# A factor of one and a half on the planned loads of MoE2's x, and the order searched anew with operations that either of two engines can take

## The chip, the cores and the metric

The kernel runs on one core of a Trainium2 chip. The metric is the device time of one execution in microseconds (us), lower is better. The five engines run their own instruction lists in order and wait for each other by semaphores: PE (TensorE, matrix products), DVE (VectorE), ACT (ScalarE), POOL (GpSimd), and SP (SyncE), which here issues nearly all DMA transfers. PEld in a profile is PE's loading of weights, which runs beside its products.

## The reference

Attention with a threshold, then two feed-forward blocks ("MoE" and "MoE2", each one expert), all in float32:

```python
scores = scale * q @ k.T                       # 4 batches, 8 heads, 576 x 576, head size 64
thresh = max(scores, -1) - tau
attn = softmax(where(scores >= thresh, scores, -1e9))
x = (attn @ v) as 2304 tokens x 512
h = x @ w1_in                                  # 512 -> 2048
x = (h * clip(h + 3, 0, 6) / 6) @ w1_out       # 2048 -> 512
h = x @ w2_in
out = (h * sigmoid(1.702 * h)) @ w2_out
```

## The kernel before

Products in float32 are made from parts in the format fp32r: each operand is split into a high part (a rounding copy, by ACT) and a low part (a subtraction, by POOL or DVE), and three products of parts (high x high, high x low, low x high) are accumulated. The first four attention units use plain float32 products, the others the split. Weights come as 64-bit patterns and are decoded first (L482: two ACT copies, three DVE operations, one POOL addition), then split (L514).

**Stages.** Attention has 16 units (4 batches x 4 pairs of heads). For a unit: scores S on PE (L663, L679, L695), maximum R on DVE (L711), threshold `th` (L712), exponential on ACT (L714), masking and sum on DVE (L715), normalisation of `e` on POOL (L728), transposition of `e` on PE (L769) with the copy to `et` on ACT (L772), product with v on PE (L811, L828), result `xr`, and its split into `xh` and `xl`. MoE1's first half of the hidden width (`moe_a`, products L888 and L913) is worked in between the units, so that PE has work while the softmax chains run. Then come the second half of MoE1 (`moe_b`, and `wide` with L1003 and L913), and MoE2 in five blocks of tokens, twice, once for each half of the hidden width. For MoE2's first product two blocks of 256 tokens and 256 columns are combined, so that seven products do instead of eight (L1101, PE line L1114); its x is read back from DRAM as two tiles, xa and xb (`halves`, L1044, loads at L1050), differences of them are made on DVE (L1056), and each of the seven operands is split (L1060: high part on ACT, low part `outlring` on DVE).

**What sets the order.** Nothing in the order is written out by hand. Each operation is added to a plan with an engine, a cost in ns, a nominal time and its buffers. `order` (L135) is a list scheduler: it plays the plan with these costs, with gaps between engines (LAT, L24), four PSUM banks, at most eight transfers at a time, and the rule that DVE and POOL do not hold their common port at once (PORT). `settle` (L260) alternates it with a backward pass, then perturbs the priorities by a list of random seeds (KICKS, SHAKES); what is left at the end is the order in which instructions are issued. A negative number in these lists exchanges an operation's engine for its alternative, where it has one (`alt`). Before the change SHAKES holds 264 seeds and no negative number. A transfer costs bytes / 360 ns (L403), with a factor for some kinds: 1.5 for weights (L504), 1.4 and 1.5 for the first k and q (L617, L614), none for MoE2's x.

**Padding.** `fill` (L290) walks through PE's planned list and, where the plan's PE stands still and a PSUM bank is free, puts in products of a constant tile `two` (L1281), which nothing reads:

```python
count = int((s - t) / 450 if s < 12000 else (s - t - 300) / 216)
```

Of the kernel before, what the change touches and what calls it, by code (L numbers as in the profile page):

```python
# [18 lines left out]
P = 128  # L19
# [37 lines left out]
)  # L57


# [275 lines left out]
def tile_top_attention_moe_moe2(  # L335
# [13 lines left out]
    nc = tc.nc  # L349
# [42 lines left out]
    def add(eng, cost, time, name, fn, rd=(), wr=(), touch=(), alt=None):  # L392
        op = pl.add(eng, cost, time, fn, rd, wr, name, touch)
        op.alt = alt
        for c, names in changed:
            if any(b.pool in names for b in op.bufs):
                op.deps.add(c)
        return op

    def move(time, name, nbytes, fn, rd=(), wr=(), eng=SP):  # L400

        op = add(eng, 590, time, name, fn, rd, wr)
        add(DMA, nbytes / 360, time, name, lambda: None, rd, wr).deps.add(op)  # L403

    def buf(tag, ring, pool, shape, dt=F32):
        return Buf(pl, tag, ring, lambda: pools[pool].tile(shape, dt, tag=tag, name=tag, bufs=ring), pool)
# [27 lines left out]
    def f32(ap):  # L434
        return ap.bitcast(F32)
# [4 lines left out]
    def act(n):  # L440
        return 51 + 0.834 * n

    def dve(n):
        return 69 + 1.042 * n
# [4 lines left out]
    def pool2(n):  # L449
        return 160 + 2.13 * n  # L450

    def copy(o, i, **kw):
        return lambda: nc.scalar.activation(out=o(), in_=i(), func=ACTF.Copy, **kw)  # L453

    def tt(eng, o, a, b, op):
        return lambda: (nc.vector if eng == DVE else nc.gpsimd).tensor_tensor(out=o(), in0=a(), in1=b(), op=op)  # L456

    dram = ctx.enter_context(tc.tile_pool(name="dram", bufs=1, space=bass.MemoryType.DRAM))
    x1d, ypd, x2d, y2d = (dram.tile([DM, NT], F32, name=n) for n in ("x1d", "ypd", "x2d", "y2d"))
# [584 lines left out]
    def halves(c0, n, whole, K):  # L1044

        T = n if whole else 2 * n
        xa, xb = (buf(x, 1, "xs", [P, 2, 512]) for x in ("xa", "xb"))
        src_b = [x2d_b[b, p] for b, p in x2d_b if b * S + CH[p][0] < c0 + T and c0 < b * S + sum(CH[p])]
        for i, x in enumerate((xa, xb)):
            move(K("LX"), "LX", 8 * P * T, lambda i=i, x=x: nc.sync.dma_start(out=x.t[:, :, :T], in_=x2d[i * 2 * P:(i + 1) * 2 * P, c0:c0 + T].rearrange("(k p) t -> p k t", p=P)), src_b, [x])  # L1050

        def part(x, i=0):
            return lambda: x.t[:, :, i:i + n]

        def minus(o, a, b, rd, wr):
            add(DVE, dve(2 * n), K("XD"), "XD", tt(DVE, o, a, b, ALU.subtract), rd, wr)  # L1056

        out_ = []

        def put(i, src, rd):  # L1060
            h, l = (buf("out" + x + "ring2", HF, "ring2", [P, DM], F32R) for x in "hl")

            def v(x):
                return x.t[:, :2 * n].rearrange("p (k n) -> p k n", k=2)

            add(ACT, 93 + act(2 * n), K("XHC") + i, "XHC", copy(lambda: v(h), src), rd, [h])
            eng = XENG[i]
            add(eng, pool2(2 * n) if eng == POOL else dve(2 * n), K("XLC") + i, "XLC", tt(eng, lambda: v(l), src, lambda: f32(v(h)), ALU.subtract), rd + [h], [l])
            out_.append((h, l))

        put(0, part(xa), [(xa, 0)])
        if whole:
            put(1, part(xb), [(xb, 0)])
            return out_
        t1, t2 = (buf("xt", 2, "xs", [P, 2, 256]) for _ in range(2))
        minus(part(t1), part(xa, n), part(xa), [xa], [t1])
        put(1, part(t1), [t1])
        put(2, part(xb), [(xb, 0)])
        minus(part(t2), part(xb, n), part(t1), [(xb, 1), t1], [t2])
        put(3, part(t2), [t2])  # L1080
        put(4, part(xb, n), [(xb, 1)])
        minus(part(xa, n), part(xa, n), part(xb, n), [(xb, 1)], [(xa, 1)])
        put(5, part(xa, n), [(xa, 1)])
        minus(part(xb), part(xb), part(t2), [t2], [(xb, 0)])
        put(6, part(xb), [(xb, 0)])
        return out_
# [65 lines left out]
    def moe2(c0, T, f0, w, t0, last):  # L1152
# [4 lines left out]
        def K(name, i=0):  # L1157
            return t0 + dt * i + NOMINAL[name]

        xs = halves(c0, n, whole, K)  # L1160
        pys = [buf(f"py{c}", 1, "py", [P, 512]) for c in range(KC)]

# [14 lines left out]
        for c in range(KC):  # L1177
# [15 lines left out]
            else:  # L1193
# [6 lines left out]
                   T=5000, DT=4000, DM=4700, EF=5400, EH=5500, EL=6000, AV=7000, RB=8500, BT=9000, XR=9400, XM=9600, XH=10000, XL=10500, ST=10000, H=0, RL=1500, GT=2000, GH=2500, GL=3000,  # L1200
# [4 lines left out]
    t, u = 0, 0  # L1205
    for b in range(B):
        halves_ = []
        for j in range(H // 2):
            halves_.append(unit(u, b, j, t))
            if u < FULL:  # L1210
                halves_[j](0)
                t, u = t + 2700 * 4, u + 1
            else:
                halves_[j]()
                t, u = t + 2700 * 9, u + 1
# [124 lines left out]
```

## Time and profile before

| | |
|---|---|
| device time, 3 runs | 1059.94 to 1062.44 us, median 1061.24 us |
| the profiled execution | 1058.04 us, span of its instructions 1056.3 us |
| busy in it | PE 1043.3, PEld 948.3, DVE 730.1, ACT 629.6, POOL 511.3 us |
| granted clock of PE | 1.00 throughout |
| DMA | 141.72 MB, 134 GB/s in the mean |

A share of busy time is a mean over stages with different limits, and PE's padding counts as busy. In the view by windows a row gives each engine's busy time and instruction count in that stretch. In a timeline each row has the start, the duration, the engine, line and operation, and in brackets the idle time before it with what ended it. A line number can be that of a helper: L453 is every ACT copy, L456 every subtraction, addition or multiplication of two tensors. One float32 product of the program leaves two rows in the trace (padding L1281, L679, L695).

### The profile page before, as it was taken

How to read it: one execution, taken by the hardware profiler on the slowest of the kernel's cores; microseconds unless marked ns; L12 is line 12 of the kernel's file. 1: busy time of each engine (PE TensorE's matmuls, PEld its weight loads, DVE VectorE, ACT ScalarE, POOL GpSimd, SP SyncE). 2: the span in 40 equal slices, each digit the busy share in tenths (PEclk: the TensorE clock that was granted, in tenths of full speed). 3: DMA queues.
4: the chain of work that ended last, by engine and by line, in shares of the span. 5: the costliest groups of instructions: out<-in, count | busy, mean ns of one | idle time of the engine just before them, and what ended most of it. 6: DMA issues, size and time to landing. Idle time of an engine off the chain costs nothing.

```text
span 1056.3 us, 19440 instructions
## 1 busy us (share of the span) xinstructions
PE 1043.3 (99%) x7084; PEld 948.3 (90%) x7084; DVE 730.1 (69%) x1502; ACT 629.6 (60%) x1240; POOL 511.3 (48%) x581
## 2 busy tenths in 40 slices
PE   8999999999999999999999999999999999999998
PEld 6687888899889998999999999889988998989988
DVE  8988888767878782688865434997687577464534
ACT  5999676666767664766553225656665576345433
POOL 4688888776867663765573217431322232001000
PEclk9999999999999999999999999999999999999999
DMA  8334565645564535455743303446554342321302
GB/s 249 102 114 141 151 172 162 184 132 164 161 184 132 152 111 162 133 148 169 229 136 124 102 28 115 134 125 204 169 181 129 125 157 77 117 85 37 95 11 66
DMA packets 83648, 141.72 MB, mean 134 GB/s; under 512 B 8160, under 2 KB 47712, under 8 KB 82016
## 3 DMA queue, kind: packets, MB, share of 16 engines
q1 hardware_dynamic: 83408, 140.18, 43.8%
q8 instruction: 56, 0.92, 0.4%
q14 instruction: 40, 0.33, 0.1%
q10 hardware_dynamic: 144, 0.29, 0.1%
HBM read 97.32 MB, written 43.12 MB: 133 GB/s over the span
## 4 chain that ended last, share of the span: by engine, by line
PE 90%; DVE 4%; POOL 3%; issue 2%; ACT 1%; DMA 0%; POOLq 0%; DVEq 0%; ACTq 0%
PE py L913 27%; PE pm L1114 16%; PE pm L888 11%; PE pm L913 8%; PE pm L1003 7%; PE pm L828 6%; PE ps L663 5%; PE pm L769 5%; PE pm L811 2%; PE ps L695 1%; POOL e L728 1%; POOL kqv L456 1%; DVE e L715 1%; DVE nm L711 1%; PE pm L1281 1%
## 5 line engine op out<-in xcount | busy, mean ns | idle before, releaser
L913 PE MATMUL py<-g,outhring 128*128 128x512 f32 (+3 forms) x1024 | 279.8, 357 | 1.8 <-DVE g L456 0.7
L913 PEld LDWEIGHTS py<-g,outhring 128*128 128x128 f32 x1024 | 177.9, 188 | 18.2 <-DVE g L456 1.9
L913 PE MATMUL py<-g,outlring 128*128 128x512 f32 (+3 forms) x512 | 182.5, 356 | 0.0
L1114 PE MATMUL pm<-outlring,inhring 128*128 128x256 f32 x512 | 144.0, 281 | 1.2 <-DVE outlring L456 1.2
L1114 PE MATMUL pm<-outhring,inhring 128*128 128x256 f32 x512 | 144.3, 282 | 0.0
L1114 PE MATMUL pm<-outhring,inlring 128*128 128x256 f32 x512 | 143.8, 281 | 0.0
L711 DVE TENSOR_REDUCE nm<-ps 128x1 f32<-128x576 f32 x144 | 107.0, 751 | 42.4 <-PE ps L663 36.4
L715 DVE SCALAR_TENSOR_TENSOR e<-ps,th,e 128x576 f32<-128x576 f32 x128 | 102.5, 811 | 17.8 <-ACT e L714 15.8
L456 POOL TENSOR_TENSOR g<-t,g 128x256 fp32r<-128x256 f32 (+2 forms) x88 | 83.4, 953 | 63.1 <-ACT g L453 50.2
L714 ACT ACTIVATE e<-ps,nm 128x576 f32<-128x576 f32 x128 | 93.2, 738 | 32.4 <-DVE nm L711 27.0
L456 POOL TENSOR_TENSOR wmstg<-wmstg,wrstg 128x512 uint32<-128x512 uint32 x48 | 65.9, 1373 | 96.3 <-DVE wmstg L510 57.6
L456 POOL TENSOR_TENSOR g<-tc,g 128x512 fp32r<-128x512 f32 x24 | 32.2, 1341 | 162.6 <-ACT g L453 160.8
L913 PE MATMUL pm<-g,outhring 128*128 128x256 f32 (+1 forms) x512 | 106.8, 300 | 0.0
L913 PEld LDWEIGHTS py<-g,outlring 128*128 128x128 f32 x512 | 96.2, 188 | 10.9
L1114 PEld LDWEIGHTS pm<-outlring,inhring 128*128 128x128 f32 x512 | 96.7, 189 | 5.4 <-DVE outlring L456 1.5
L1114 PEld LDWEIGHTS pm<-outhring,inhring 128*128 128x128 f32 x512 | 96.7, 189 | 4.6 <-ACT u L453 0.4
L888 PE MATMUL pm<-xh,inhring 128*128 128x256 f32 (+1 forms) x320 | 97.5, 305 | 0.2
L1114 PEld LDWEIGHTS pm<-outhring,inlring 128*128 128x128 f32 x512 | 97.5, 190 | 0.0
L888 PE MATMUL pm<-xh,inlring 128*128 128x256 f32 (+1 forms) x320 | 94.5, 295 | 0.0
L888 PE MATMUL pm<-xl,inhring 128*128 128x256 f32 (+1 forms) x320 | 94.4, 295 | 0.0
L772 ACT ACTIVATE et<-pm 128x512 f32<-128x512 f32 (+2 forms) x144 | 75.1, 557 | 17.1 <-PE pm L769 14.6
L913 PEld LDWEIGHTS pm<-g,outhring 128*128 128x128 f32 x512 | 82.1, 189 | 0.5 <-issue 0.5
(122 smaller groups left out, 2461.1 us busy)
## 6 DMA issues: line engine op xcount, KB each, us to landing
turned<-tr SPq DMA_DIRECT2D x12, 1024.0 KB, 3.9
et<-turned SPq DMA_DIRECT2D x48, 256.0 KB, 6.2
wrawstg<-in_w1i_dram SPq DMA_DIRECT2D x16, 512.0 KB, 4.0
wrawstg<-in_w1o_dram SPq DMA_DIRECT2D x16, 512.0 KB, 3.6
wrawstg<-in_w2i_dram SPq DMA_DIRECT2D x16, 512.0 KB, 4.2
wrawstg<-in_w2o_dram SPq DMA_DIRECT2D x16, 512.0 KB, 4.1
qk<-in_k_dram SPq DMA_DIRECT2D x24, 288.0 KB, 3.6
qk<-in_q_dram SPq DMA_DIRECT2D x24, 288.0 KB, 3.8
```

Of the source, the lines that this page charges most:

```text
L456: return lambda: (nc.vector if eng == DVE else nc.gpsimd).tensor_tensor(out=o(), in0=a(), in1=b(), op=op)
L663: nc.tensor.matmul(ps.t[:, i, :SH], qss[hd].t[:, q0:q0 + P], w[hd].t[:, i * SH:(i + 1) * SH], start=a, stop=z)
L711: add(DVE, 672, K("R", s), "R", lambda: nc.vector.tensor_reduce(out=nm.t[:, c], in_=ps.t[:, :, :SH], op=ALU.max, axis=AX.XY, negate=True), ...
L714: add(ACT, 624, K("X", s), "X", lambda: nc.scalar.activation(out=ev(), in_=ps.t[:, :, :SH], func=ACTF.Exp, bias=nm.t[:, c]), [ps, (nm, s)] ...
L715: add(DVE, 736, K("M", s), "M", lambda: nc.vector.scalar_tensor_tensor(out=ev(), in0=ps.t[:, :, :SH], scalar=th.t[:, c], in1=ev(), op0=ALU ...
L769: nc.tensor.transpose(pt.t[:kn, o:o + P], e_of[s].t[:, keys(k)], id_b.t)
L772: add(ACT, act(size), K("EH", at), "EH", lambda: nc.scalar.activation(out=dst(kn)[0], in_=dst(kn)[1](pt.t[:kn, :size]), func=ACTF.Copy), [ ...
L828: nc.tensor.matmul(pv[p].t[64 * hd:64 * hd + 64, :CH[p][1]], v_(k, hd), x, start=k == 0, stop=k == 4)
L888: nc.tensor.matmul(ph.t[:, :n], a, v, start=(cc == 0 and i == 0), stop=(cc == KC - 1 and i == 2))
L913: nc.tensor.matmul(py.t[:, :n], a, v, start=(st and i == 0), stop=(sp and i == 2))
L1003: nc.tensor.matmul(ph.t[:, :n], a, v, start=(cc == 0 and q == 0), stop=(cc == KC - 1 and q == 2))
L1114: nc.tensor.matmul(o.t[:, :n], u.t[:, ws], v.t[:, xv], start=(st and kk == 0 and i == 0), stop=(sp and kk == 1 and i == 2), skip_group_che ...
```

## The change

The cost of the two loads of x for each MoE2 block is multiplied by 1.5 in the plan; the transfers are the same. SHAKES keeps its 264 seeds and gets 319 numbers more, of which 136 are negative: they exchange engines, some operations more than once, and 108 operations end on their alternative engine.

```diff
@@ SHAKES
-    461089389, 641840093, 940935001, 302617623, 395272555, 1040798833, 496012712, 151625592, 914921461,
+    461089389, 641840093, 940935001, 302617623, 395272555, 1040798833, 496012712, 151625592, 914921461, 827017900, -3099, -737, -1052, 639256428, 818694334, 148551951,
...
@@ halves
-            move(K("LX"), "LX", 8 * P * T, lambda i=i, x=x: nc.sync.dma_start(
+            move(K("LX"), "LX", 8 * P * T * 1.5, lambda i=i, x=x: nc.sync.dma_start(
...
```

In the built program DVE goes from 1360 instructions to 1390, ACT from 1243 to 1235, POOL from 586 to 564, SP stays at 487, and PE has 56 padding products where it had 34. Lines of the changed kernel are 18 higher than those of the kernel before.

**Start, DVE's list.** Rows around the seventh and eighth score tiles; before:

```order
L711 TENSOR_REDUCE nm<-ps 128x1
L715 SCALAR_TENSOR_TENSOR e,sm<-ps,th,e 128x576
L712 TENSOR_SCALAR th<-nm,nt 128x1
L623 TENSOR_SCALAR kqv<-kqv,sc 128x384
L507 TENSOR_SCALAR wmstg<-wmstg 128x512
L619 TENSOR_SCALAR g<-g,sc 128x512
L715 SCALAR_TENSOR_TENSOR e,sm<-ps,th,e 128x576
L711 TENSOR_REDUCE nm<-ps 128x1
L509 TENSOR_SCALAR wmstg<-wmstg 128x512
L712 TENSOR_SCALAR th<-nm,nt 128x1
```

The same place in the changed kernel:

```order
L729 TENSOR_REDUCE nm<-ps 128x1
L733 SCALAR_TENSOR_TENSOR e,sm<-ps,th,e 128x576
L730 TENSOR_SCALAR th<-nm,nt 128x1
L791 COPY et<-pm 128x512
L525 TENSOR_SCALAR wmstg<-wmstg 128x512
L733 SCALAR_TENSOR_TENSOR e,sm<-ps,th,e 128x576
L729 TENSOR_REDUCE nm<-ps 128x1
L740 RECIPROCAL rc<-sm 128x4
L527 TENSOR_SCALAR wmstg<-wmstg 128x512
L729 TENSOR_REDUCE nm<-ps 128x1
```

A copy of transposed `e` out of PSUM, which ACT made before, stands in DVE's list, and a threshold is missing from it (it is on ACT).

**Entry into MoE2, POOL's list.** `g<-t` are low parts of MoE1, `g<-tc` those of MoE2, `inlring` low parts of weights; before:

```order
L456 TENSOR_TENSOR g<-t_849,g 128x432
L456 TENSOR_TENSOR inlring_8183<-ws,inhring_8161 128x512
L456 TENSOR_TENSOR inlring_8271<-wmstg_8052,inhring_8180 128x256
L456 TENSOR_TENSOR inlring_8182<-wmstg_8063,inhring_8160 128x512
L456 TENSOR_TENSOR g<-tc,g 128x512
```

The same place in the changed kernel:

```order
L474 TENSOR_TENSOR g<-t_872,g 128x432
L474 TENSOR_TENSOR wmstg_8111<-wmstg_8111,wrstg_8180 128x512
L474 TENSOR_TENSOR g<-tc,g 128x512 x2
L474 TENSOR_TENSOR inlring_8458<-wmstg_8096,inhring_8442 128x256
L474 TENSOR_TENSOR inlring_8456<-wmstg_8111,inhring_8405 128x512
L474 TENSOR_TENSOR inlring_8457<-ws,inhring_8425 128x512
```

The three low parts of the last pair of weights stand behind the first two `g` of MoE2, no longer ahead of them.

**Entry into MoE2, SP's list** of transfers; before:

```order
L496 DMA wrawstg_8019<-in_w2i_dram 128x4x256
L496 DMA wrawstg_8087<-in_w2o_dram 128x1024
L496 DMA wrawstg_8109<-in_w2o_dram 128x1024
L1050 DMA xa<-x2d 128x2x512
L1050 DMA xb<-x2d 128x2x512
```

The same place in the changed kernel:

```order
L514 DMA wrawstg_8067<-in_w2i_dram 128x4x256
L514 DMA wrawstg_8130<-in_w2o_dram 128x1024
L1068 DMA xa<-x2d 128x2x512
L1068 DMA xb<-x2d 128x2x512
L514 DMA wrawstg_8185<-in_w2o_dram 128x1024
```

The loads of the first block's x have moved ahead of one load of weights.

## Rows read from the trace of the kernel before

**Rows 1.** The page's first part: busy time, share of the span, instructions.
```profile
PE 1043.3 (99%) x7084; PEld 948.3 (90%) x7084; DVE 730.1 (69%) x1502; ACT 629.6 (60%) x1240; POOL 511.3 (48%) x581
```

**Rows 2.** Windows: length, then busy (count) of PE, PEld, DVE, ACT, POOL; clock; DMA.
```profile
0.00:5.00 5.00, 3.62 (x17) 3.62 (x18) 1.25 (x9) 1.28 (x1) 3.99 (x20) 1.00 0.40 115
5.00:54.30 49.30, 46.33 (x295) 33.76 (x294) 46.91 (x116) 39.77 (x73) 26.77 (x35) 1.00 0.60 179
54.30:420.00 365.70, 363.30 (x2767) 319.25 (x2768) 273.06 (x679) 254.20 (x499) 269.56 (x364) 1.00 0.53 152
420.00:650.00 230.00, 229.64 (x1420) 225.58 (x1418) 143.32 (x240) 113.70 (x217) 120.22 (x98) 1.00 0.44 133
650.00:750.00 100.00, 97.36 (x651) 90.72 (x650) 81.93 (x142) 62.86 (x129) 36.37 (x27) 1.00 0.48 150
750.00:1053.00 303.00, 302.96 (x1942) 275.36 (x1940) 183.23 (x318) 157.73 (x323) 54.40 (x41) 1.00 0.32 103
1053.00:1056.30 3.30, 0.10 (x1) 0.00 (x0) 0.42 (x1) 0.00 (x0) 0.00 (x0) 1.00 0.24 79
```

**Rows 3.** Windows of the padding (L1281) alone: length, then PE and PEld busy.
```profile
0.00:5.00 5.00, 3.62 (x16) 3.49 (x16) 1.00 0.40 115
5.00:54.30 49.30, 4.04 (x29) 3.59 (x28) 1.00 0.60 179
54.30:420.00 365.70, 3.48 (x24) 3.19 (x24) 1.00 0.53 152
```

**Rows 4.** The chain that ended last, around 37 and 54 us: start, length, what.
```profile
37.31 0.14 DVE th L712
37.46 1.21 PE ps L679 x4
...
54.30 2.06 PE pm L888 x15
```

**Rows 5.** Timeline of DVE at the start, between 27 and 31 us.
```profile
27.90 0.68 DVE L510 SCALAR_TENSOR_TENSOR wmstg<-wrawstg,wmstg 128x512 uint32<-128x512 uint32 x1
28.50 0.81 DVE L715 SCALAR_TENSOR_TENSOR e<-ps,th,e 128x576 f32<-128x576 f32 x1
...
29.91 0.42 DVE L507 TENSOR_SCALAR wmstg<-wmstg 128x512 f32<-128x512 f32 x1
30.24 0.21 DVE L712 TENSOR_SCALAR th<-nm,nt 128x1 f32<-128x1 f32 x1
30.36 0.41 DVE L456 TENSOR_TENSOR xr<-xr,pm 128x256 f32<-128x256 f32 x1
```

**Rows 6.** Timelines of DVE and of POOL around 24 us.
```profile
23.78 1.43 DVE L623 TENSOR_SCALAR kqv<-kqv,sc 128x384 f32<-128x384 f32 x1
...
23.50 1.49 POOL L456 TENSOR_TENSOR inlring<-wmstg,inhring 128x512 fp32r<-128x512 f32 x1 [0.92 <-ACT inhring L453]
```

**Rows 7.** Timelines of SP, ACT, DVE, POOL and PE at the entry into MoE2.
```profile
659.86 0.38 SPq L1050 DMA_DIRECT2D xa<-x2d  x1
...
665.20 0.63 ACT L453 ACTIVATE outhring<-xa 128x512 fp32r<-128x512 f32 x1 [1.16 <-DMA xa<-x2d]
...
667.62 1.76 DVE L456 TENSOR_TENSOR outlring<-xt,outhring 128x512 fp32r<-128x512 f32 x1
669.31 0.68 DVE L456 TENSOR_TENSOR outlring<-xb,outhring 128x512 fp32r<-128x512 f32 x1
...
666.22 2.62 POOL L456 TENSOR_TENSOR inlring<-wmstg,inhring 128x256 fp32r<-128x256 f32 x2 [1.68 <-ACT inhring L453]
...
669.44 0.39 PE L1114 MATMUL pm<-outlring,inhring 128*128 128x256 f32 x1 [1.23 <-DVE outlring L456]
```

**Rows 8.** The view of tile xa: time from issue to landing of its ten loads.
```profile
DMA to landing us min/median/max: 2.8/3.8/5.3
```

**Rows 9.** Who PE waited for from 54.3 to 420 us: total, times, longest.
```profile
PE pm L769 <- ACT et L772: 0.9, 2, 0.7
PE pm L769 <- POOL e L728: 0.5, 2, 0.3
```

More of the change, by code (lines that the diff above doesn't have):

```diff
@@ L1049, in halves @@
         for i, x in enumerate((xa, xb)):
-            move(K("LX"), "LX", 8 * P * T, lambda i=i, x=x: nc.sync.dma_start(out=x.t[:, :, :T], in_=x2d[i * 2 * P:(i + 1) * 2 * P, c0:c0 + T].rearrange("(k p) t -> p k t", p=P)), src_b, [x])
+            move(K("LX"), "LX", 8 * P * T * 1.5, lambda i=i, x=x: nc.sync.dma_start(out=x.t[:, :, :T], in_=x2d[i * 2 * P:(i + 1) * 2 * P, c0:c0 + T].rearrange("(k p) t -> p k t", p=P)), src_b, [x])
         def part(x, i=0):
```

18 rows, old and new, of the table SHAKES are left out of this document.

## Prediction

> **What bounds the kernel now.** I read the page's line of busy times first, then the window view by stage, the padding alone in the same windows, the chain, and last the timelines of the two places where TensorE stands still. TensorE (PE) is busy for 1043.3 of the 1056.3 us [rows 1], and no operation of PE's real work is touched by the change. What an order can win is only what PE does not spend on that work: 1056.3 - 1043.3 = 13.0 us of idle time, and the padding matmuls on `two`, which count as busy. The window view splits the idle time: 1.4 us before the first matmul, 3.0 us from 5 to 54.3 us, 2.4 us from 54.3 to 420, 0.4 us from 420 to 650, 2.6 us from 650 to 750, nothing from 750 to 1053, and 3.2 us behind the last matmul [rows 2]. Padding adds 3.6, 4.0 and 3.5 us in the first three stretches [rows 3]. Head, first loads and tail (1.4 + 3.6 + 3.2) no order removes. So three places count: the start with 7.0 us, the attention stage with 5.9 us, the entry into MoE2 with 2.6 us. They cannot give more than about 16 us together, and the last 300 us give nothing, though x of MoE2 is loaded there for six more blocks.
>
> At the start the chain runs through VectorE's (DVE's) list until 37.5 us and then through PE, up to the first matmul of MoE1 at 54.3 us [rows 4]. DVE is busy for 46.9 of the 49.3 us before that matmul, ScalarE (ACT) for 39.8 [rows 2]. An operation that joins DVE there delays nearly everything behind it.
>
> At the entry PE waits 1.23 us for a low half of x that DVE makes. That subtraction took 1.76 us, the next one of the same size 0.68, and GpSimd (POOL) ran two weight subtractions, 2.62 us together, over just that time. Before it, ACT waited 1.16 us for xa [rows 7].
>
> **The change part by part.** The added factor changes no transfer; it alters what the plan believes, and with the new numbers the whole program is put into another order. What can be costed is what stands in the orders.
>
> *Entry into MoE2.* xa is issued at 659.86, before and after the change behind the last weights of w2i; but in the new order one of the two w2o loads stands behind xa and xb, not ahead. ACT got xa at 665.20, 5.3 us after its issue [rows 7]; the ten loads of xa took 2.8 to 5.3 us with a median of 3.8 [rows 8], so up to 1.5 us comes back there. POOL's two subtractions that blocked DVE now stand behind two `g` of MoE2, which cannot run before the first products are done. PE has three more output matmuls as cover, too. The 1.23 us should vanish, and about half of the remaining 1.4 us of that stretch is of the same chain: I take a quarter of it, 0.35. Term: **-1.6 us**, ends -2.6 (all idle time of the stretch) and 0 (the load is still late).
>
> *Start.* Up to the fourth `xr` multiply, which releases MoE1's first matmul, DVE has the same list as before but for these: two copies of 128x512 out of PSUM and one of 64x128 come from ACT, one subtraction of 128x512 comes from POOL, one cast of 128x512 comes from ACT, and three thresholds `th` of 128x1 go to ACT. DVE's step is read from start to start: an operation of 128x512 on two inputs 0.60 us, a one-input operation of that size 0.33, `th` 0.12 [rows 5]. The copies' PSUM source is not in these rows, so I price them like the 0.60 and the small one at 0.2, between `th` and 0.33. Sum: 3 x 0.60 + 0.33 + 0.2 - 3 x 0.12 = **+2.0 us**. What hid the copies before was ACT, idle for 9.5 of those 49.3 us; that cover is spent for nothing by moving them to the fuller engine. Lower end 0: ACT's share shrinks by as much, and if it was ACT that held the pace anywhere, DVE's idle 2.4 us take the rest. Upper end from the padding: the new order has 37 padding matmuls ahead of MoE1's first one, the old 22. The program puts one only where the plan's PE stands still, and each leaves two rows in the trace: 29 rows took 4.04 us [rows 3], 0.14 us a row, so 15 x 2 x 0.14 = +4.2 us.
>
> The rows show that a DVE operation can be held by POOL: a scaling of `kqv` took 1.43 us while POOL subtracted for 1.49 us [rows 6], against 0.42 for a one-input operation of 512 elements [rows 5]. The Trainium skill, SBUF — State Buffer, section SBUF: two separate sides, has the rule: DVE and GpSimd share one pair of ports under an exclusive lock, and DVE operations in a two-port mode or with two SBUF inputs wait for the whole GpSimd instruction. By it the two newcomers at the start with SBUF sources alone could each wait about 1.0 us (1.43 - 0.42), and the start would cost +4.0 instead of +2.0; the trace agrees with the rule at these places. I keep +2.0, because moving the subtraction also takes 1.3 us of work from POOL there, and the sum's upper end holds the other value anyway.
>
> *Attention stage, 54.3 to 420 us.* In the whole program 32 `th` move from DVE to ACT; 13 copies of transposed `e`, 27 other copies and casts, two scalings, 10 normalisations and 14 subtractions move to DVE; four clamps of weights go from DVE to POOL. Most of this lies in this stage. DVE is the fuller helper here (273 us of 366, against 254 and 270 [rows 2]) and has room for them. What PE visibly waited for is an ACT copy of `et` (0.9 us) and a POOL normalisation (0.5 us) [rows 9], the very kinds that are moved. A `th` on ACT is not in the trace; it lies off PE's path unless it delays an exponential. So stalls may shrink; but padding in this stage rises from 12 to 19 matmuls, 7 x 2 x 0.14 = 2.0 us more, which speaks for as many or more voids in the plan. I take **0**; ends -3.0 (half of 2.4 idle + 3.5 padding) and +2.0.
>
> *Rest.* 420 to 650 and 750 to 1053 hold 0.4 us of idle time [rows 2]: 0. The later loads of x are hidden now, and earlier issue of them wins nothing.
>
> Sum: -1.6 + 2.0 + 0 = **+0.4 us**. The profiled execution took 1058.04 us (span 1056.3 and 1.7 around it) and becomes 1058.4; it was 3.2 us quicker than the median of the runs, 1061.24, so for that median the forecast is **1061.6 us**: no change that can be told, since a measurement of this kernel separates some 0.2%, 2.1 us.
>
> **Rivals.** *The search helps the attention stage.* Moving the waited-for copies and normalisations takes half of that stage's 5.9 us (-3.0), the entry gives -1.6, the start costs only +1.0 because ACT is relieved: -3.6, **1057.6**. For it: the visible waits are of those kinds [rows 9]. Against: more padding, and DVE is the helper that gets the work.
>
> *The plan is emptier: slower.* All 22 additional padding matmuls stand in voids that exist on the chip, most at the start: 22 x 2 x 0.14 = +6.2, less 1.6 at the entry: +4.6, **1065.8**. It decides from the point where MoE1's first matmul comes after about 57 us instead of 54.3. For it: DVE is nearly full at the start, and PE from 54.3 us on has so little idle time that a late start is not caught up. Against: the padding rounds, and some voids may have been too short to be padded before.
>
> *The loads of x come no earlier:* the entry keeps its 2.6 us of idle time, and only the start's price is left: +2.0, **1063.2**, on the edge of what can be told. For it: the first xa is held by the room it needs, not by the plan's belief; against: the weights moved out of its way.
>
> **How the numbers follow.** No change 0.36, faster by the attention stage 0.33, slower by the emptier plan 0.23, no earlier loads 0.08. The last two give slower 0.31, if I count the last case on that side. The range goes from 1055.3 (-5.9: start 0, entry -2.6, attention -3.3, a little past its end) to 1067.4 (+6.2, the padding with no gain at the entry).
>
> **What would show it.** MoE1's first matmul at 56 to 57 us; PE idle under 1.5 us from 650 to 750 and no subtraction of 1.7 us on DVE at the entry; idle and padding together near 6 us between the start and 420 us; nothing new after 750. I am wrong if MoE1 starts at 54 us or earlier, if it starts after 58, or if the deferred weight subtractions on POOL make PE wait near 690 us.

## The result, and the profile after

| | before | changed |
|---|---|---|
| device time, median of 5 runs each | 1061.24 us | 1068.98 us (1067.71 to 1071.07) |
| ratio | 1 | 1.0077, 95% interval 1.0061 to 1.0093 |
| the profiled execution | 1058.04 us, span 1056.3 | 1067.71 us, span 1065.9 |

The change is slower by 0.8 %, outside the predicted range. The granted clock is not the reason: it was 1.000 in the profiled execution, and the changed kernel's two runs with 1.000 took 1067.71 and 1068.09 us, its three with 0.998 took 1068.98 to 1071.07. The page's busy times of the changed kernel, to be held against [rows 1]:

```profile
PE 1048.5 (98%) x7128; PEld 953.5 (89%) x7128; DVE 756.4 (71%) x1532; ACT 617.7 (58%) x1232; POOL 502.8 (47%) x559
```

To find the place, both traces are cut at the same points of the program: MoE1's first product (L888, now L906), the first and last score product L663 (now L681), the first product of the second half of MoE1's output, the first `wide` product, MoE2's first product, PE's end. The windows of the changed kernel at these points (columns as in [rows 2]):

```profile
0.00:5.00 5.00, 3.62 (x19) 3.62 (x20) 1.35 (x9) 1.28 (x1) 3.94 (x18) 1.00 0.41 112
5.00:58.40 53.40, 49.36 (x322) 37.09 (x320) 50.18 (x118) 38.33 (x71) 27.79 (x36) 1.00 0.56 166
58.40:104.60 46.20, 45.88 (x343) 36.53 (x344) 41.73 (x96) 41.10 (x84) 39.58 (x47) 1.00 0.41 121
104.60:410.00 305.40, 301.48 (x2306) 269.27 (x2305) 247.66 (x591) 199.05 (x402) 212.22 (x291) 1.00 0.54 156
410.00:480.40 70.40, 70.34 (x534) 67.34 (x533) 40.83 (x70) 42.12 (x85) 43.04 (x37) 1.00 0.47 134
480.40:529.20 48.80, 46.47 (x339) 45.25 (x338) 38.48 (x76) 26.86 (x54) 27.01 (x21) 1.00 0.54 166
...
678.90:1062.70 383.80, 381.59 (x2500) 349.10 (x2499) 256.32 (x452) 208.68 (x433) 77.61 (x56) 1.00 0.35 113
```

Padding alone (L1299, was L1281) in the changed kernel, as in [rows 3]:

```profile
0.00:5.00 5.00, 3.62 (x18) 3.44 (x18) 1.00 0.41 112
5.00:58.40 53.40, 7.66 (x57) 7.12 (x56) 1.00 0.56 166
...
104.60:410.00 305.40, 4.54 (x32) 4.13 (x32) 1.00 0.54 156
```

```profile
410.00:480.40 70.40, 0.83 (x6) 0.78 (x6) 1.00 0.47 134
```

The kernel before, cut at its own times of the points that [rows 2] doesn't have:

```profile
54.30:100.60 46.30, 45.96 (x339) 36.06 (x339) 39.46 (x99) 42.19 (x85) 38.95 (x46) 1.00 0.43 127
100.60:401.20 300.60, 298.54 (x2285) 266.85 (x2286) 231.20 (x575) 203.38 (x396) 225.73 (x312) 1.00 0.54 156
401.20:471.30 70.10, 70.10 (x533) 67.64 (x533) 38.40 (x65) 43.74 (x93) 39.15 (x35) 1.00 0.49 141
471.30:519.90 48.60, 48.24 (x360) 47.96 (x359) 41.28 (x79) 29.06 (x59) 25.96 (x21) 1.00 0.60 184
...
666.60:1053.10 386.50, 383.81 (x2506) 349.96 (x2505) 254.15 (x445) 210.39 (x435) 78.81 (x58) 1.00 0.35 113
```

A stretch's length less PE's busy time is idle time; idle time and padding together are what PE does not spend on real work:

| stretch | before: idle + padding | changed: idle + padding | difference |
|---|---|---|---|
| to MoE1's first product | 4.35 + 7.66 = 12.0 | 5.42 + 11.28 = 16.7 | +4.7 |
| on to the last score product | 2.40 + 3.48 = 5.9 | 4.24 + 4.54 = 8.8 | +2.9 |
| on to the first `wide` product | 0.36 + 0 = 0.4 | 2.39 + 0.83 = 3.2 | +2.8 |
| MoE2 to PE's end | 2.69 | 2.21 | -0.5 |

The sum, +9.9 us, is about the growth of the span (+9.6). The stretch that the table leaves out, from the first `wide` product to MoE2's first, has neither idle time nor padding in either kernel; it is longer by 3.0 us because 18 more products stand in it, which in the kernel before stand ahead of it. Half of the loss lies ahead of 58.4 us; MoE2, where the factor stands, gained half a microsecond.

What PE waited for in the changed kernel (total, times, longest), the costliest:

```profile
PE py L931 <- DVE g L474: 2.3, 2, 1.6
PE ps L681 <- DVE e L733: 1.7, 1, 1.7
...
PE pm L787 <- DVE e L733: 1.4, 1, 1.4
PE pm L787 <- ACT et L790: 1.2, 3, 0.7
PE py L931 <- DVE yc L1212: 0.9, 1, 0.9
PE pm L1132 <- DVE c L474: 0.8, 1, 0.8
```

All of these but one end on DVE. Timeline of DVE in the changed kernel while the start falls behind (in the kernel before the sixteenth maximum `nm` was taken at 41.1 us, here at 46.58):

```profile
43.04 1.00 DVE L525 TENSOR_SCALAR wmstg<-wmstg 128x512 f32<-128x512 f32 x1
43.97 0.41 DVE L541 CAST inhring<-wmstg 128x512 fp32r<-128x512 f32 x1
44.30 0.42 DVE L527 TENSOR_SCALAR wmstg<-wmstg 128x512 uint32<-128x512 uint32 x1
44.63 1.43 DVE L641 TENSOR_SCALAR kqv<-kqv,sc 128x384 f32<-128x384 f32 x1
45.98 0.68 DVE L528 SCALAR_TENSOR_TENSOR wmstg<-wrawstg,wmstg 128x512 uint32<-128x512 uint32 x1
```

Timeline of POOL over the same time:

```profile
42.47 1.30 POOL L474 TENSOR_TENSOR wmstg<-wmstg,wrawstg 128x512 uint32<-128x512 uint32 x1 [2.06 <-DVE wmstg L528]
44.46 1.39 POOL L474 TENSOR_TENSOR inlring<-wmstg,inhring 128x512 fp32r<-128x512 f32 x1 [0.70 <-DVE inhring L541]
```

The scaling at 43.04 takes 1.00 instead of 0.42 us and ends 0.27 us after POOL's addition; that of `kqv` at 44.63 takes 1.43 and ends 0.21 us after POOL's subtraction. DVE is held until POOL's operation is over, as at 23.78 us in [rows 6], but here more often: six operations lose 3.6 us in this way ahead of MoE1's first product, in the kernel before two lose 1.2. The groups of the three decode operations of a weight tile on DVE show it as a mean (instructions, busy us, mean ns). They are cut at the fourth multiply of `xr`, which releases MoE1's first product; the kernel before, to 52.08 us:

```profile
L510 DVE SCALAR_TENSOR_TENSOR wmstg<-wrawstg,wmstg 128x512 uint32<-128x512 uint32 x7 | 4.8, 688 | 0.0
L509 DVE TENSOR_SCALAR wmstg<-wmstg 128x512 uint32<-128x512 uint32 x7 | 3.0, 422 | 0.1
L507 DVE TENSOR_SCALAR wmstg<-wmstg 128x512 f32<-128x512 f32 x7 | 2.9, 419 | 0.3 <-ACT wmstg L506 0.3
```

The changed kernel, to 56.57 us:

```profile
L528 DVE SCALAR_TENSOR_TENSOR wmstg<-wrawstg,wmstg 128x512 uint32<-128x512 uint32 x7 | 4.8, 679 | 0.0
L525 DVE TENSOR_SCALAR wmstg<-wmstg 128x512 f32<-128x512 f32 x7 | 4.4, 632 | 0.7 <-ACT wmstg L524 0.7
L527 DVE TENSOR_SCALAR wmstg<-wmstg 128x512 uint32<-128x512 uint32 x7 | 4.2, 595 | 1.6 <-POOL wmstg L526 1.6
...
L791 DVE COPY et<-pm 128x512 f32<-128x512 f32 x2 | 1.4, 680 | 0.0
L474 DVE TENSOR_TENSOR inlring<-wmstg,inhring 128x512 fp32r<-128x512 f32 x1 | 0.7, 684 | 0.0
```

Seven of each stand ahead of that multiply in both kernels. The scalings (`TENSOR_SCALAR`) are longer by 0.17 x 7 + 0.21 x 7 = 2.7 us in sum, and DVE waits 1.6 us for a clamp of weights that went to POOL.

The wait of 1.6 us in the table of waits is of the same kind. DVE, then POOL, around 496.5 us in the changed kernel:

```profile
496.44 1.95 DVE L474 TENSOR_TENSOR g<-t,g 128x320 fp32r<-128x320 f32 x2
```

```profile
496.67 1.38 POOL L474 TENSOR_TENSOR wmstg<-wmstg,wrstg 128x512 uint32<-128x512 uint32 x1 [1.76 <-ACT wmstg L524]
```

Two subtractions for which PE waits, about 0.48 us each where nothing holds them, take 1.95 us together because the second one meets an addition on POOL: it ends 0.3 us after it.

### The profile page after: what moved, and what is told of

It reads as the page before. It is cut to its first block, busy times and chain, and to the rows that moved or that the text cites. A ratio compares the mean times of both kernels' runs of the same rounds, so it can differ in the third digit from the quotient of the medians.

```text
span 1065.9 us, 19497 instructions
## 1 busy us (share of the span) xinstructions
PE 1048.5 (98%) x7128; PEld 953.5 (89%) x7128; DVE 756.4 (71%) x1532; ACT 617.7 (58%) x1232; POOL 502.8 (47%) x559
## 4 chain that ended last, share of the span: by engine, by line
PE 84%; DVE 7%; ACT 3%; DMA 2%; POOL 2%; issue 1%; SPq 1%; DVEq 0%; ACTq 0%; POOLq 0%
PE py L931 26%; PE pm L1132 15%; PE pm L906 10%; PE pm L931 8%; PE pm L1021 7%; PE ps L681 6%; PE pm L846 6%; PE pm L787 4%; DVE wmstg L528 1%; PE pm L829 1%; PE ps L713 1%; DMA wrawstg<-in_w1i_dram 1%; DVE nm L729 1%; DMA kqv<-in_vp_dram 1%; DVE wmstg L527 1%
## 5 line engine op out<-in xcount | busy, mean ns | idle before, releaser
L474 POOL TENSOR_TENSOR g<-t,g 128x432 fp32r<-128x432 f32 (+2 forms) x84 | 81.5, 974 | 65.3 <-ACT g L471 48.3
L906 PE MATMUL pm<-xh,inhring 128*128 128x256 f32 (+1 forms) x320 | 97.6, 305 | 0.2
L906 PE MATMUL pm<-xh,inlring 128*128 128x256 f32 (+1 forms) x320 | 94.5, 295 | 0.0
L906 PE MATMUL pm<-xl,inhring 128*128 128x256 f32 (+1 forms) x320 | 94.4, 295 | 0.0
L681 PE MATMUL ps<-kqv 128*128 128x288 f32 x480 | 80.9, 300 | 1.7 <-DVE e L733 1.7
```

What stands on the lines that cost most here:

```text
L681: nc.tensor.matmul(ps.t[:, i, :SH], qss[hd].t[:, q0:q0 + P], w[hd].t[:, i * SH:(i + 1) * SH], start=a, stop=z)
L906: nc.tensor.matmul(ph.t[:, :n], a, v, start=(cc == 0 and i == 0), stop=(cc == KC - 1 and i == 2))
```

## The experiments

**Theories.** *A*: the factor throws the search back. A number's draw hits a stretch of the plan that is worked out from the planned length and times, so under other planned times the 264 old numbers move other operations than those they were picked for; the 319 new ones win a part of it back, and the loss is the order's. *B*: the exchanged operations cost it. *A1* is A with the exchanges paying their own durations at the start. *C*: the longer planned loads cost it, by what they displace around MoE2. In the edits, `chain(factor, numbers)` stands for the loops of `settle`: it returns the last priorities, the exchanged operations and the planned start times. `flip` exchanges operations, and `self.lx` holds the planned loads of x.

### The factor and the numbers, taken apart

**The factor with the old numbers.** SHAKES of the changed kernel, cut:

```diff
-    461089389, ..., 914921461, 827017900, -3099, -737, ...
+    461089389, ..., 914921461,
```

> The factor of 1.5 with the 264 old numbers only, and so no exchanged operation. Three theories. (A) The factor alone throws the search back: each number's draw goes to a stretch of the plan that is worked out from the planned length and the planned times, so with other planned times the 264 old numbers move other operations than those they were picked for, and the new numbers win only a part of that back. Then this kernel is far slower than both: its plan holds 138 padding products where the kernel before has 34 and the changed kernel 56, and 104 more of them at 2 rows of 0.14 us are +29 us, so 1080 to 1095 us, most of it idle time and padding in the attention stage. (B) The exchanged operations cost the time (work moved to DVE at the start, thresholds moved to ACT): without them the time is that of the kernel before, 1059 to 1064 us. (C) The longer planned loads of x themselves cost it, by what they displace around MoE2: 1067 to 1071 us, with the loss behind 600 us.

Measured: 1098.15 us (one run), 37.7 more than the kernel before beside it (1060.42): A. Its windows from 65 to 432.4 us, first all instructions, then padding alone:

```profile
65.00:432.40 367.40, 357.76 (x2705) 314.68 (x2705) 267.42 (x656) 241.51 (x474) 262.33 (x353) 1.00 0.50 145
```

```profile
65.00:432.40 367.40, 13.44 (x94) 12.66 (x94) 1.00 0.50 145
```

In the attention stage alone 9.6 us of idle time and 13.4 us of padding, where the kernel before has 2.4 and 3.5.

**The new numbers with the old planned loads.**

```diff
-            move(K("LX"), "LX", 8 * P * T * 1.5, ...
+            move(K("LX"), "LX", 8 * P * T, ...
```

> All 583 numbers of the changed kernel, exchanges included, with the factor left at 1.0: the mirror image of the factor with the old numbers. By A the new numbers, picked under the longer planned loads, fit the old planned lengths as badly as the old numbers fit the new ones: 130 padding products, 96 more than the kernel before at 2 rows of 0.14 us are +27 us: 1080 to 1100 us. If the longer planned loads are the loss (C), taking them away brings 1059 to 1063 us.

Measured: 1103.6 us (one run). Shorter planned loads do not help these numbers, they spoil them: A, and against C. Numbers and planned times belong together.

**The factor with the priorities kept.**

```diff
+        key, flipped, _ = self.chain(1.0, SHAKES[:264])
+        for op in self.lx:
+            op.cost = self.lxsize[op] * 1.5
         self.link()
         self.order(key)
```

> The priorities are those that the kernel before ends with (searched with the factor 1.0 and the 264 old numbers); the factor of 1.5 is put on the loads of x only for the last pass that makes the order; no operation is exchanged. By theory A (the search is thrown back) the factor costs nothing where the priorities are kept: 1059 to 1063 us, ratio to the kernel before 0.998 to 1.002. By B (exchanged operations) the same. By C (the longer planned loads) 1065 to 1071 us.

Measured: 1059.94 us, ratio 0.9995 (0.9984 to 1.0007). The factor costs nothing where it does not reach the search; C falls. Its trace says more than its total. The window from its MoE2's first product to PE's end, and the costliest wait of PE that is new:

```profile
668.93:1053.70 384.77, 383.89 (x2510) 350.23 (x2508) 252.27 (x446) 210.56 (x434) 80.44 (x57) 1.00 0.35 113
```

```profile
PE pm L864 <- ACT kqv L489: 1.5, 1, 1.5
```

PE stands idle for 0.88 us there, against 2.69 in the kernel before: at the place that it is made for, the factor alone is worth 1.8 us. Between MoE1's first product and the first `wide` one, idle time grew from 2.8 to 4.6 us, which takes it back.

**The changed kernel without its exchanges.**

```diff
-    461089389, ..., 914921461, 827017900, -3099, -737, -1052, 639256428, ...
+    461089389, ..., 914921461, 827017900, 639256428, ...
```

> The changed kernel without the 136 negative numbers: the factor of 1.5 and the 264 old and 183 new seeds, and the plan made from them, every operation on its old engine. By A (the search is thrown back and the new numbers win only part back) slower than the changed kernel, since 183 numbers were picked for a plan with exchanges: 76 padding products where the kernel before has 34, 42 more of 2 rows of 0.14 us, +12 us: 1068 to 1077 us. By B 1059 to 1064 us.

Measured: 1078.34 us (one run), 9 slower than the changed kernel. Against B: without exchanges the other new numbers are worth less, not more. This run and the two single runs above came out 1 to 4 us over A's ranges.

### Where in the program

Both kernels' plans are joined: operations that one plan starts before a point keep its order and engines, the others take priorities and engines of the other plan.

```diff
+        key, flipped, _ = self.chain(1.5, SHAKES)
+        head, moved, start = self.chain(1.0, SHAKES[:264])
+        early = {o.n for o in self.ops if start[o.n] < edge}
+        key = [start[n] - 1e9 if n in early else k for n, k in enumerate(key)]
+        flipped = {n for n in flipped if n not in early} | {n for n in moved if n in early}
```

> The order and the engines of the kernel before for everything planned earlier than 40 us ahead of MoE2's first product; behind that the priorities, the exchanged operations and the factor of the changed kernel. By A the loss lies in the order of the start, the attention and MoE1, and the entry into MoE2 gave 0.5 us back: 1059 to 1062.5 us, ratio 0.998 to 1.001, MoE1's first product at 54.3 us and a wait under 1 us at the entry into MoE2 where the kernel before has 1.23. By C, which puts the loss on the longer planned loads, 1064 us or more. If exchanged operations cost time wherever they are (B), the 40 or so that lie behind this point make it slower than the kernel before by 1 to 3 us.

Measured: 1058.78 us, ratio 0.9986 (0.9975 to 0.9997): a little faster than the kernel before, by an interval that only just leaves out 1, and the best version of this study. MoE1's first product came at 54.9 us. So the order, the exchanges and the planned loads that the change brings behind 620 us are not the loss.

> The reverse: the order and the exchanged operations of the changed kernel up to 40 us ahead of MoE2's first product, then the priorities, the engines and the planned loads of the kernel before. By A it keeps the whole loss ahead of MoE2 and loses the gain at the entry: 1068 to 1072 us, ratio 1.006 to 1.010, MoE1's first product at 58 us. By C, 1060 to 1064 us.

Measured: 1070.78 us, ratio 1.0093 (1.0079 to 1.0107), MoE1's first product at 59.6 us. The whole loss lies ahead of MoE2, as the table by stretches says.

With the point at MoE1's first product:

> The order and engines of the kernel before up to MoE1's first product, behind it the priorities, the exchanged operations and the factor of the changed kernel. If the 4.7 us that the changed kernel loses at the start simply add to the rest, MoE1's first product comes at 54 to 55 us and the whole takes 1064 to 1066 us, ratio 1.003 to 1.005. If the priorities of the rest fit only the start they were searched with, the gain is lost again in the attention stage: 1067 to 1071 us.

Measured: 1068.02 us, ratio 1.0076 (1.0058 to 1.0094). The start was on time, and the rest lost it again. Windows of this kernel from its first MoE1 product (54.7 us) on:

```profile
54.70:103.26 48.56, 46.58 (x336) 35.76 (x337) 42.94 (x97) 40.85 (x84) 39.05 (x45) 1.00 0.42 124
103.26:410.60 307.34, 304.37 (x2323) 270.56 (x2322) 249.33 (x592) 198.26 (x402) 212.46 (x291) 1.00 0.54 154
```

PE stands idle for 1.98 us in the first of them, against 0.32 in the changed kernel (46.20 - 45.88), and 307.34 us pass in the second, against 305.40. The priorities of the rest fit the start with which they were searched. An early start is worth something only if the order behind it can use it.

### The order or the engines

Here nothing is planned anew: the list of operations stays, and only the engine of exchanged operations is set back, or set, in its place.

```diff
         self.order(key)
+        self.flip(flipped)
         return sorted(self.ops, key=lambda o: (self.start[o.n], o.n))
```

> The list of operations in the order of the changed kernel, unchanged; but the 108 exchanged operations run in their places on the engines that they had before. Nothing is planned anew. Theory A1: the loss is the order's (which operation stands behind which, and which decode operations of DVE meet a subtraction on POOL), with the exchanges paying only their own durations at the start: 1065 to 1069 us, MoE1's first product at 56 to 57 us, for the exchanged operations add 2.35 us to DVE's busy time ahead of it in the traces (copies 1.36, 0.28, 0.28 and 0.41, a subtraction 0.68, less 0.66 of thresholds). Theory B: the exchanged operations are the loss everywhere: 1059 to 1063 us. A third outcome, over 1071 us, would say that the exchanges are what makes this order work at all.

Measured: 1071.13 us, ratio 1.0102 (1.0087 to 1.0117), MoE1's first product at 59.7 us. The old engines in the new order win nothing back. B falls, and so does the small gain that A1 foresaw. The expectation's third outcome, over 1071 us, is reached by 0.1 us, and the interval overlaps that of the changed kernel; that the exchanges make this order work is not shown.

> The order of the kernel before, unchanged, with the 108 operations run in their places on the engines that the changed kernel gives them. By A1 (the order) 1060 to 1064 us: a little slower from work that comes where the order has no room for it, MoE1's first product at 55 to 56.5 us. By B (the exchanged operations) 1067 to 1071 us.

Measured: 1076.93 us, ratio 1.0163 (1.0149 to 1.0177), over what either theory said; MoE1's first product at 60.6 us. The exchanges alone, in an order that was not made for them, cost more than the whole change. A part of it goes with the granted clock, which was 0.993 to 0.998 in these five runs (1079.27 us at 0.993, 1075.69 at 0.998). The exchanges cost time in a foreign order; in their own, taking them away gains nothing.

Only the exchanges of the start, undone in place:

```diff
+        edge = min(self.start[o.n] for o in self.ops if o.name == "H" and o.eng == PE)
+        self.flip({n for n in flipped if self.start[n] < edge})
```

> The changed kernel's order, with only those exchanged operations undone in place that are planned ahead of MoE1's first product (three thresholds, three copies out of PSUM, two casts, a subtraction, a clamp). MoE1's first product came at 58.4 us in the changed kernel and at 54.3 in the one before. If the exchanges are half of it (their 2.35 us of DVE work), it comes at 56 to 57 us and the whole takes 1066 to 1068 us; if they are all of it, 54 to 55 us and 1063.5 to 1065.5; if the order's own pace is all of it, 58 to 59 us and 1068 to 1070.

Measured: 1069.28 us, ratio 1.0084 (1.0070 to 1.0098), MoE1's first product at 59.1 us. Some 2.4 us of work left DVE, 0.4 came back to it with the clamp, and the wait for the clamp went; the start came no earlier. The holds did not shrink: by the groups, 4.3 us where the changed kernel has 3.7. Nor did DVE's idle time, 3.6 us against 3.2, though the 1.6 us for the clamp are gone from it. Groups of this kernel, 5 to 59 us:

```profile
L546 DVE SCALAR_TENSOR_TENSOR wmstg<-wrawstg,wmstg 128x512 uint32<-128x512 uint32 x8 | 6.8, 849 | 0.0
L543 DVE TENSOR_SCALAR wmstg<-wmstg 128x512 f32<-128x512 f32 x8 | 5.8, 725 | 0.3 <-ACT wmstg L542 0.3
```

The hold of `kqv` at 44.63 us, for one, only moved to another operation. Timeline of DVE, then POOL, in this kernel:

```profile
45.71 0.41 DVE L659 TENSOR_SCALAR kqv<-kqv,sc 128x384 f32<-128x384 f32 x1
46.04 1.76 DVE L546 SCALAR_TENSOR_TENSOR wmstg<-wrawstg,wmstg 128x512 uint32<-128x512 uint32 x1
```

```profile
45.79 1.46 POOL L492 TENSOR_TENSOR inlring<-wmstg,inhring 128x512 fp32r<-128x512 f32 x1 [0.74 <-ACT inhring L489]
```

The scaling began just ahead of POOL's subtraction and took 0.41 us instead of 1.43; the two-input decode operation behind it met the subtraction and took 1.76 instead of 0.68.

### The holds, taken away

Ahead of MoE1's first product POOL's additions of weights write 16 columns instead of 512, and its subtractions are replaced by a fill with zeros.

```diff
+            if n and op == ALU.subtract:
+                nc.gpsimd.memset(f32(o()), 0.0)
+            else:
+                (nc.vector if eng == DVE else nc.gpsimd).tensor_tensor(out=o()[:, :n], in0=a()[:, :n], in1=b()[:, :n], op=op)
```

> The changed kernel; ahead of MoE1's first product, the additions and the subtractions of weights on POOL are left out for all but 16 columns (the additions) or replaced by a fill with zeros (the subtractions), so part of MoE1's weights is wrong. What this takes away is the time in which a DVE operation is held until such a POOL operation ends: at the start 6 DVE operations took 3.6 us over the usual duration of their kind in the changed kernel, 2 took 1.2 us over it in the kernel before. If these holds are what makes the start late, MoE1's first product comes at 55 to 56 us (58.4 with the holds) and the whole takes 1065 to 1067 us. If the start is late because of the order alone, it stays at 57.5 to 58.5 us, 1068 to 1070 us.

> The same edit in the kernel before, for comparison: part of MoE1's weights is wrong. By its 1.2 us of holds MoE1's first product, at 54.3 us, can come at most 1.2 us earlier: 53 to 54.3 us and 1059 to 1061 us.

Measured: the changed kernel 1066.88 us, ratio 1.0063 (1.0043 to 1.0082), MoE1's first product at 56.4 instead of 58.4 us; the kernel before 1060.14 us, ratio 0.9992 (0.9978 to 1.0005), first product at 54.0 instead of 54.3. The scalings of the changed kernel are short again:

```profile
L565 DVE TENSOR_SCALAR wmstg<-wmstg 128x512 uint32<-128x512 uint32 x8 | 3.9, 482 | 1.6 <-POOL wmstg L564 1.6
L563 DVE TENSOR_SCALAR wmstg<-wmstg 128x512 f32<-128x512 f32 x7 | 3.0, 425 | 0.0
```

Of the 4.1 us by which the start is late, the holds are about 1.7 (2.0 less the 0.3 that the kernel before gains by the same edit). The edit also shortens POOL's own work, from 27.8 to 16.1 us ahead of MoE1's first product, so a part of the 1.7 can be POOL's results coming sooner. The other 2.4 us stay. This kernel still has the newcomers on DVE and, like the changed one, the 1.6 us in which DVE waits for a clamp on POOL; no run takes both the holds and the exchanges away, so how the 2.4 us divide is not shown.

**Padding.** `fill` without products behind the first 12 us of the plan:

```diff
-                count = int((s - t) / 450 if s < 12000 else (s - t - 300) / 216)
+                count = int((s - t) / 450 if s < 12000 else 0)
```

> The changed kernel without its padding products behind the first 12 us of its plan (they feed nothing). If padding only fills time in which PE would wait, the time stays at 1067 to 1071 us, with idle time in its place and the granted clock at 1.0. If the padding itself holds PE's own work back, up to the 8.9 us it takes come back: 1060 to 1066 us. If it keeps the clock up, a granted clock under 1.0 at the start and over 1072 us.

Measured: 1066.65 us, ratio 1.0061 (1.0041 to 1.0082), not to be told from the changed kernel's 1.0077 (1.0061 to 1.0093); MoE1's first product at 58.2 us, the mean granted clock 0.998. The padding mostly fills waits; it is the sign of the loss, not its cause.

### Numbers picked in the old plan

1232 more numbers, 16 of them exchanges, each kept only if it made the plan of the kernel before no longer:

```diff
+        key, flipped, _ = self.chain(1.0, SHAKES[:264])
+        ref = key
+        for seed in MORE:
+            if seed < 0:
+                flipped ^= {-seed}
+            else:
+                key = kicked(key, length, seed, kinds, len(names), ref)
```

> The plan of the kernel before with its lengths (factor 1.0) and its 264 numbers, and on top of it 1232 further numbers picked one at a time for a shorter plan, 16 of them exchanges of an operation's engine; 31 padding products where the kernel before has 34. By A (numbers and exchanges are harmless where they are picked in the plan they act on) 1057 to 1061.5 us, ratio 0.997 to 1.001. If exchanged operations or many further numbers cost time on the chip that the plan does not see (B), 1063 to 1069 us.

Measured: 1065.0 us, ratio 1.0045 (1.0030 to 1.0061). Against my expectation: an order that the plan counts as shorter is slower on the chip. With its 16 exchanges undone in place:

> The order of the run with numbers picked on the old plan, unchanged, its 16 exchanged operations back on their old engines in their places. If the exchanges cost its 4.3 us (B), 1059 to 1062 us. If the order costs it, which the plan counts as shorter than it is on the chip, 1063 to 1068 us.

Measured: 1064.37 us, ratio 1.0037 (1.0023 to 1.0051). It is the order again, not the exchanges. The costliest of PE's waits there that is new against the kernel before:

```profile
PE pm L1267 <- ACT p L605: 1.5, 3, 0.9
```

So theory A holds with an addition: besides numbers that do not fit the planned times, the plan itself does not see everything that the chip does, and picking further in it does not need to pay. This wait is in MoE2, but MoE2 as a whole idles no longer than before (2.4 us against 2.7); between MoE1's first product and the first `wide` one PE idles for 4.2 us against 2.8. Which of the plan's assumptions is off stays open.

## Why the prediction was wrong

**Start, +2.0 us forecast, +4.7 measured.** This is the step that failed first. The term priced what moved between the engines and put at nothing what the new order does to the operations that stayed on DVE. The count of the moved ones was right: up to the fourth multiply of `xr`, which comes at 56.57 us instead of 52.08, the groups show 1.4 + 0.3 + 0.7 + 0.4 us for those that joined DVE, less 0.7 for three thresholds: 2.1 us. The rest of the list is the same up to there, as the prediction says, but it stands in another order opposite POOL's additions and subtractions: the scalings of weights that were on DVE all along are longer by 2.7 us, and the clamp that went to POOL makes DVE wait for 1.6 us, also put at nothing. That is 6.4 us together; the rest of the list gave some 1.9 back. Nor did the moved operations decide it: undone in place, they gave nothing back. The rule of the Trainium skill, SBUF — State Buffer, section SBUF: two separate sides, on the exclusive lock of the shared ports gave +4.0, and I set it aside. The trace and the run without the holds agree with it in kind (1.7 us), but it did not strike the two newcomers that I had named (0.4 and 0.7 us, undisturbed); it struck operations that had stood on DVE all along. That +4.0 lies near the measured +4.7 is luck. The upper end from the padding, +4.2, was passed by 0.5: padding stands where the plan is empty, and idle time stands beside it. By its own sign, a start after 58 us, the prediction is wrong.

**Attention, 0 forecast with ends -3.0 and +2.0, +2.9 measured.** I had seen the seven more padding products and still let the moved copies and normalisations weigh against them. PE's waits for `et` did not shrink (1.2 us, three of them, against 0.9 [rows 9]), and one of 1.7 us for `e` on DVE came in.

**Rest, 0 forecast, +2.8 measured between 410 and 529 us,** 2.3 of it in two waits for `g`. The stage had 0.4 us of idle time, and I took this to mean that nothing could be lost there. A stage without idle time bounds what an order can win, not what it can lose.

**Entry into MoE2, -1.6 forecast, -0.5 measured.** The wait of 1.23 us for `outlring` and the next one went, as said; new waits of 0.5 to 0.9 us for `u`, `yc` and `c` took their place between 686 and 777 us. The factor on the kept priorities took 1.8 us of idle time away there, so the term fits the factor; the new order did not keep it. Joined to the old head, this part gave the only gain.

**The rivals.** "The plan is emptier: slower" had the mechanism's sign, its place and its point of decision (MoE1's first product after 57 us). Its price was too low: the padding grew by 5.5 us in the trace (11.1 to 16.7), near the 6.2 that it said, but the idle time grew by 4.5 beside it. What I missed is the reason behind it: a factor in a planned cost is not a local edit when the order hangs on numbers picked under that cost. "The loads of x come no earlier" did not decide anything; that the later loads of x are hidden was right: no wait of PE for a load stands there.

## What to carry to other kernels

Where an order is made by a list of picked numbers, a changed cost makes all of them mean something else; put the new cost on the kept priorities (here 0.9995), or keep the old order up to the place that the change is for and take the new one behind it (here 0.9986). The padding in the plan tells a thrown-back order in advance: in four versions each padding product beyond the old count went with 0.35 to 0.45 us of device time (7.7 / 22, 37.7 / 104, 17.9 / 42, 42.9 / 96); between nearly equal plans it tells nothing, 31 products were slower than 34. And where one engine paces a stage, compare its whole list with what runs opposite to it on the engine whose operations hold it, not only the operations that moved.

## What was not expected of the hardware

A fill on POOL holds DVE too, though it reads nothing, and the hold goes both ways. A scaling on DVE in the kernel before, then POOL's fills around it:

```profile
5.48 0.66 DVE L619 TENSOR_SCALAR g<-g,sc 128x512 f32<-128x512 f32 x1 [0.19 <-DMA g<-in_q_dram]
```

```profile
4.93 0.14 POOL L613 MEMSET kqv<- 64x64 f32 x1
5.12 0.74 POOL L592 MEMSET et<- 64x640 f32 x1
5.80 0.42 POOL L613 MEMSET kqv<- 64x64 f32 x1
```

The scaling took 0.66 us, where the two others of its kind took 0.48, and ended 0.28 us after the fill in which it began, about as long after it as the scaling at 43.04 us above ended after an addition. The small fill at 5.80 us ended 0.08 us after the scaling and took 0.42 us, against 0.14 for the one at 4.93. So the fills with zeros in the run without the holds shorten a hold (0.53 us each, where a subtraction takes 1.39) and do not forbid it.

One difference between executions has nothing to do with the order: products with 432 columns took 355 ns in the kernel before and 358 in three other runs, over whole stretches; one of the three is the kernel before without the holds, whose order is the same there. The groups from 520 to 668 us of the kernel before, then of the run with numbers picked in the old plan:

```profile
L1003 PE MATMUL pm<-xh,inhring 128*128 128x432 f32 x128 | 45.4, 355 | 0.0
```

```profile
L1154 PE MATMUL pm<-xh,inhring 128*128 128x432 f32 x128 | 45.8, 358 | 0.0
```

There are 768 such products. They overlap, so what counts is how far apart they start: 193 ns in the one, 196 in the other, some 2 us in sum. Single profiles of these kernels cannot be compared more closely than that.
